# One load of the output weights in 30 KB rows instead of fifteen pieces in 2 KB rows, with O gathered through GpSimd

## The chip, the cores, the metric

One core of one Trainium2 chip. The metric is the device time of one execution in microseconds (us). Most executions of a kernel agree within 0.3%. The "span" is the stretch that the profile covers; it is 1 to 2 us shorter than the time.

## The reference

Decode attention with a cache, then a gated feed-forward layer, two batch rows, bfloat16:

```python
# B=2, Sq=1, D=512, H=32 heads, Sk=8192 cached keys, Dh=128, F=1376
q = layernorm(x) @ wq                       # wq 512 x 4096
p = softmax(q @ k_cache^T * Dh**-0.5)       # k_cache, v_cache: 2 x 32 x 8192 x 128, 134 MB each
h = x + (p @ v_cache) @ wo                  # wo 4096 x 512, 4.2 MB
n = layernorm(h)
out = h + (relu(n @ W_gate) * (n @ W_up)) @ W_down
```

Nearly all bytes are the two caches. wo is 1.5% of the 281 MB, and it is wo that the change is about.

## The kernel before

Work goes in 32 "pairs" p (two heads of one batch row: one K tile and one V tile of 4 MB each, four slots in SBUF). Two pairs make a round g. For each pair, VectorE computes 96 of the 128 columns of scores (a product of K with the query, then halving additions); TensorE computes the other 32 by transposing K and multiplying with the query. ScalarE takes exponentials, TensorE multiplies with V. After each round, O of two heads is normalized and multiplied with 256 rows of wo. SyncE issues all loads, in one queue, as slots come free. The loads of a round, and the GpSimd copy that lets TensorE begin on a K tile:

```python
def load_wo(dst, g, sem):                   # 256 KB: 128 partitions, 2 KB each
    nc.sync.dma_start(dst[:], A_wo[2*g*Dh:2*(g+1)*Dh].rearrange("(p r) n -> p (r n)", r=2)).then_inc(sem, 16)
...
for p in range(NP):
    ...
    if p < P0:                              # P0 = the last pair but one
        nc.gpsimd.wait_ge(slot_sem[s], 16 * (g + 1))                  # K has landed
    nc.gpsimd.tensor_copy(out=q2c[p % 2][:], in_=q2[:, p]).then_inc(g2p, 1)   # TensorE waits for g2p
    ...
    dve.wait((slot_sem[s], 16 * (g + 1)), t_q_b)
    t_dm[p] = dve.run(nc.vector.tensor_tensor(out=prod[:, 0:jd, :], in0=k_t[:, 0:jd, :], in1=qv, op=ALU.mult))
    ...                                     # 4 halving additions between prod and tb, 1 reduction
    if p + 2 < NP:
        sp.wait(t_dm[p], tokp("pt", p, NG - 1))     # product and transposes of K(p) done
        load(s, A_k_cache, p + 2)
    if p % 2 == 1 and 1 <= g < NI:
        sp.wait(tok("om", g))
        load_wo(wo_cur, g, sem_wo)
    if p < NP - 4:
        sp.wait(tokp("pv", p))
        load((2 * p + 1) % 4, A_v_cache, p + 2)
```

After the last V come the loads of W_up, W_gate and W_down, and the kernel ends with a serial stretch: collect O, project with the last 256 rows of wo, layernorm, up, gate, down, output.

The softmax here doesn't subtract the row's maximum and nothing guards it: scores larger than these inputs give would overflow.

## Time and profile before

| what | value | where it is read |
|---|---|---|
| time | 662.9 us (662.8 to 663.1) | runs |
| span | 661.1 us | profile |
| busy: DMA queue / DVE / PE | 99.3% / 70% / 51% | page, parts 3 and 1 |
| DMA rate | 425 GB/s mean, about 430 in the middle | page, part 2 |
| granted TensorE clock | mostly 0.5 or 0.6 of full speed after the first 83 us | page, part 2 |

The page of the kernel before: busy time of the engines, the DMA rows of the 40 slices (tenths of busy time; GB/s), the hardware queue, and the two lines of the chain that ended last.

```profile
PE 338.1 (51%) x3685; PEld 219.1 (33%) x3685; DVE 465.6 (70%) x274; ACT 198.3 (30%) x416; POOL 194.1 (29%) x48
...
DMA  9999999999999999999999999999999999999996
GB/s 381 429 426 439 421 438 429 434 424 430 438 430 428 428 430 440 427 431 428 428 438 430 428 430 430 437 427 428 429 434 432 432 424 432 436 419 442 430 419 276
...
q1 hardware_dynamic: 12664, 281.06, 99.3%
...
DMA 71%; DVE 23%; PE 2%; POOL 2%; ACT 1%; issue 0%; SPq 0%; DVEq 0%; POOLq 0%
DMA slot<-in_A_k_cache_dram 64%; DVE prod L474 14%; DVE tb L482 6%; DMA slot<-in_B_W_gate_dram 4%; DVE prod L482 3%; POOL q2c L463 2%; DMA slot<-in_A_wq_dram 2%; PE T L325 1%; PE W L229 1%; ACT q_b L276 0%; PE O L271 0%; ACT kT L499 0%; PE 
```

The queue is full from the first slice to the last but one. The last line lists whose work the chain is made of: besides the K tiles, the load of W_gate has 4% of it, so the end of the program hangs on that load. What shortens the span must therefore shorten the queue's work, or the stretch after the queue has run empty.

The timeline of the kernel before (start, duration, engine, line, operation, out<-in; in brackets how long the engine had been idle and what ended that): three products of K tiles, and two query copies.

```profile
221.96 6.56 DVE L474 TENSOR_TENSOR prod<-slot,q_b 128x12288 bf16<-128x12288 bf16 x1 [5.78 <-DMA slot<-in_A_k_cache_dram]
222.06 6.51 POOL L463 COPY q2c<-q 128x8 bf16<-128x8 bf16 x1 [13.59 <-DMA slot<-in_A_k_cache_dram]
...
241.40 6.56 DVE L474 TENSOR_TENSOR prod<-slot,q_b 128x12288 bf16<-128x12288 bf16 x1 [2.54 <-DMA slot<-in_A_k_cache_dram]
...
261.50 6.56 DVE L474 TENSOR_TENSOR prod<-slot,q_b 128x12288 bf16<-128x12288 bf16 x1 [5.78 <-DMA slot<-in_A_k_cache_dram]
```
```profile
24.10 0.19 POOL L463 COPY q2c<-q 128x8 bf16<-128x8 bf16 x1 [19.24 <-DMA slot<-in_A_k_cache_dram]
```

A product starts when its K tile lands. From 221.96 to 241.40 the queue moved V and K, 8.39 MB in 19.44 us: 431 GB/s. From 241.40 to 261.50 it moved V, K and one piece of wo, and took 20.10 us. The piece cost 0.66 us. The second fence shows a query copy with VectorE at rest, 0.19 us. Beside the product it takes 6.51 us and ends when the product ends.

The end of the kernel before: the load of W_gate (KB, and us from issue to landing), then from its timeline the last matmuls that can run without W_gate, the gate matmuls, and the last operation of VectorE.

```profile
slot<-in_B_W_gate_dram SPq DMA_DIRECT2D x1, 1376.0 KB, 29.1
...
654.15 0.41 PE L595 MATMUL T<-ident,hb 128*2 128x32 bf16 x16
...
654.71 1.71 PE L584 MATMUL O<-d_b,slot 128*128 128x2 bf16 x44
...
658.36 0.35 DVE L643 SCALAR_TENSOR_TENSOR o_r<-O,r,h_r 128x128 bf16<-128x128 f32 x1 [1.37 <-PE O L636]
```

W_gate lands at 654.66 (issued at 625.56, and 29.1 us to landing). TensorE had finished everything else at 654.56. So the serial work of the end is hidden behind the queue, but by only 0.1 us in this profile.

### The profile page before, as it was taken

The numbers are of one execution on the slowest core, as the hardware profiler recorded it, in microseconds if no ns is written. First come the engines' busy times: TensorE is split into PE (matmuls) and PEld (weight loads), VectorE is DVE, ScalarE is ACT, GpSimd is POOL, SyncE is SP. The second block draws the span as 40 slices with busy tenths as digits, with TensorE's granted clock in tenths as the row PEclk, the third lists the DMA queues.
The fourth block names the chain that finished last, engine by engine and source line by source line (L and its number), as shares of the span: only waits on it lengthen the run. The fifth ranks groups of instructions, "written<-read, shape, count | busy, mean of one in ns | idle before, by whom it ended". The sixth has DMA issues, their size and how long they took to land.

```text
span 661.1 us, 8515 instructions
## 1 busy us (share of the span) xinstructions
PE 338.1 (51%) x3685; PEld 219.1 (33%) x3685; DVE 465.6 (70%) x274; ACT 198.3 (30%) x416; POOL 194.1 (29%) x48
## 2 busy tenths in 40 slices
PE   2635554446545445644536545445653536544767
PEld 2413432324333233432314333223432314333444
DVE  1766787767688676787767688676788767688681
ACT  0603332223332123332223332123332213332360
POOL 2021333332233331233332133332233332134000
PEclk9999966656555566555655555566555665556556
DMA  9999999999999999999999999999999999999996
GB/s 381 429 426 439 421 438 429 434 424 430 438 430 428 428 430 440 427 431 428 428 438 430 428 430 430 437 427 428 429 434 432 432 424 432 436 419 442 430 419 276
DMA packets 12689, 281.22 MB, mean 425 GB/s; under 512 B 1442, under 2 KB 1540, under 8 KB 3972
## 3 DMA queue, kind: packets, MB, share of 16 engines
q1 hardware_dynamic: 12664, 281.06, 99.3%
q8 instruction: 6, 0.10, 0.1%
q14 instruction: 7, 0.06, 0.0%
q10 hardware_dynamic: 12, 0.00, 0.0%
HBM read 281.05 MB, written 0.00 MB: 425 GB/s over the span
## 4 chain that ended last, share of the span: by engine, by line
DMA 71%; DVE 23%; PE 2%; POOL 2%; ACT 1%; issue 0%; SPq 0%; DVEq 0%; POOLq 0%
DMA slot<-in_A_k_cache_dram 64%; DVE prod L474 14%; DVE tb L482 6%; DMA slot<-in_B_W_gate_dram 4%; DVE prod L482 3%; POOL q2c L463 2%; DMA slot<-in_A_wq_dram 2%; PE T L325 1%; PE W L229 1%; ACT q_b L276 0%; PE O L271 0%; ACT kT L499 0%; PE O L584 0%; PE O L636 0%; PE S L313 0%
## 5 line engine op out<-in xcount | busy, mean ns | idle before, releaser
L463 POOL COPY q2c<-q 128x8 bf16<-128x8 bf16 x32 | 190.4, 5949 | 415.5 <-DMA slot<-in_A_k_cache_dram 384.2
L474 DVE TENSOR_TENSOR prod<-slot,q_b 128x12288 bf16<-128x12288 bf16 (+1 forms) x32 | 207.7, 6491 | 128.9 <-DMA slot<-in_A_k_cache_dram 127.3
L325 PE MATMUL T<-ident_f,slot 128*128 128x128 f32 x528 | 136.5, 426 | 219.8 <-POOL q2c L463 217.8
L499 ACT ACTIVATE kT<-T 128x1024 bf16<-128x1024 bf16 x132 | 131.4, 1022 | 388.9 <-PE T L325 385.0
L325 PEld LDWEIGHTS T<-ident_f,slot 128*128 128x128 f32 x528 | 98.3, 219 | 233.6 <-POOL q2c L463 231.4
L482 DVE TENSOR_TENSOR tb<-prod 128x6144 bf16<-128x6144 bf16 (+1 forms) x64 | 136.8, 2137 | 2.2
L343 PE MATMUL O<-slot,e 128*32 128x512 bf16 x1024 | 115.5, 615 | 18.7 <-ACT e L429 18.7
L482 DVE TENSOR_TENSOR prod<-tb 128x3072 bf16<-128x3072 bf16 (+1 forms) x64 | 73.4, 1148 | 2.2
L313 PE MATMUL S<-q2c,kT 128*128 128x4 bf16 x1056 | 50.3, 170 | 37.7 <-ACT kT L499 37.7
L313 PEld LDWEIGHTS S<-q2c,kT 128*128 128x128 bf16 x1056 | 44.0, 108 | 67.8 <-ACT kT L499 65.8
L343 PEld LDWEIGHTS O<-slot,e 128*32 128x32 bf16 x1024 | 32.4, 132 | 76.6 <-issue 53.8
L355 PE MATMUL Ob<-sel,os_sb 128*64 128x2 f32 x544 | 31.1, 245 | 26.2 <-ACT os_sb L507 25.5
L355 PEld LDWEIGHTS Ob<-sel,os_sb 128*64 128x64 f32 x544 | 29.7, 217 | 28.1 <-ACT os_sb L507 26.9
L487 DVE TENSOR_REDUCE scores<-prod 128x96 f32<-128x768 bf16 (+1 forms) x32 | 30.2, 945 | 1.1
L429 ACT ACTIVATE e<-scores 64x96 bf16<-64x96 f32 (+1 forms) x64 | 19.6, 307 | 22.8 <-DVE scores L487 22.1
L438 DVE TENSOR_REDUCE zr<-Ob 128x2 f32<-128x4 f32 x15 | 2.4, 162 | 28.1 <-PE Ob L355 28.1
L429 ACT ACTIVATE e<-S 64x32 bf16<-64x32 f32 (+1 forms) x64 | 13.0, 204 | 14.8 <-PE S L313 14.5
L429 ACT ACTIVATION_READ_ACCUMULATOR e<-S 64x1 f32 x64 | 12.9, 201 | 0.7
L429 ACT ACTIVATION_READ_ACCUMULATOR e<-scores 64x1 f32 x64 | 11.8, 184 | 0.0
L507 ACT ACTIVATE os_sb<-O 128x512 f32<-128x512 f32 x16 | 9.6, 597 | 0.4
L276 ACT ACTIVATE q_b<-O 128x512 bf16<-128x512 f32 x8 | 4.3, 595 | 16.9 <-PE O L271 16.9
L234 DVE CAST qT<-W 128x64 bf16<-128x64 f32 x1 | 0.2, 224 | 11.2 <-PE W L229 11.2
(74 smaller groups left out, 72.0 us busy)
## 6 DMA issues: line engine op xcount, KB each, us to landing
slot<-in_A_k_cache_dram SPq DMA_DIRECT2D x32, 4096.0 KB, 28.1
slot<-in_A_v_cache_dram SPq DMA_DIRECT2D x31, 4096.0 KB, 31.3
slot<-in_A_wq_dram SPq DMA_DIRECT2D x1, 4096.0 KB, 12.3
slot<-in_A_v_cache_dram SPq DMA_DIRECT2D x2, 2048.0 KB, 29.6
wo_cur<-in_A_wo_dram SPq DMA_DIRECT2D x15, 256.0 KB, 27.0
slot<-in_B_W_up_dram SPq DMA_DIRECT2D x1, 1376.0 KB, 26.2
slot<-in_B_W_gate_dram SPq DMA_DIRECT2D x1, 1376.0 KB, 29.1
slot<-in_B_W_down_dram SPq DMA_DIRECT2D x2, 512.0 KB, 30.3
```

The costliest lines, as they stand in the source:

```text
L229: i = nc.tensor.matmul(Wp[:, h * B:(h + 1) * B], lhsT=wq[:, c, h * Dh:(h + 1) * Dh], rhs=lT[:, c * B:(c + 1) * B], start=(c == 0), stop=(c ...
L313: i = nc.tensor.matmul(Sp[p % 2][:, 2 * jj:2 * jj + 4], lhsT=kv_[:, k, r, :], rhs=q2c[p % 2][:, r, :], start=(r == 0), stop=(r == 1))
L325: i = nc.tensor.transpose(Tp[g % 2][:, k * 128:(k + 1) * 128], k_t[:, j:j + 2, :].rearrange("p j d -> p (j d)").bitcast(F32), ident_f[:])
L343: i = nc.tensor.matmul(Op[0][c:c + 32, :], lhsT=e_t[q][:, j // VJ, :], rhs=v_t[:, j:j + VJ, :].rearrange("p j d -> p (j d)"), start=(q == ...
L355: i = nc.tensor.matmul(Ob[64 * a_:64 * a_ + 64, B * r:B * r + B], lhsT=os_sb[:].rearrange("p (j d r) -> p j r d", j=VJ, r=2)[:, jj, r, :], ...
L429: i = nc.scalar.activation(out=e_t[q][h, j0 // VJ:j1 // VJ, 8 * q:8 * q + 8].rearrange("p g (j a) -> p g j a", a=2)[:, :, :, a], in_=src(h ...
L463: nc.gpsimd.tensor_copy(out=q2c[p % 2][:], in_=q2[:, p]).then_inc(g2p, 1)
L474: t_dm[p] = dve.run(nc.vector.tensor_tensor(out=prod[:, 0:jd, :], in0=k_t[:, 0:jd, :], in1=qv, op=ALU.mult))
L482: dve.run(nc.vector.tensor_tensor(out=o, in0=cur[:, :, 0:half], in1=cur[:, :, half:w], op=ALU.add))
L487: t_s[p] = dve.run(nc.vector.tensor_reduce(out=sc[:, 0:jd], in_=cur, axis=AX.X, op=ALU.add))
L499: to_pe(nc.scalar.activation(out=kT[gg % 2][:], in_=Tp[gg % 2][:].bitcast(BF16), func=ACT.Copy))
L507: to_pe(nc.scalar.activation(out=os_sb[:], in_=Op[0][:], func=ACT.Copy))
```

## The change

The intent: fifteen pieces of wo in 2 KB rows become one load near the start, 128 rows of 30 KB. Row p of that load holds rows 30p to 30p+29 of wo, so O has to be brought into the same order. GpSimd "spreads" O of each round into a masked tile, TensorE gathers it in PSUM over all rounds with a selector, and 30 matmuls of 512 columns do the whole projection near the end. Also: queries are copied a pair ahead, the halving additions work in place, O comes out of 4 matmuls instead of 16, and the program no longer stands in a block of its own. The core of the diff, cut:

```diff
-                    if p % 2 == 1 and 1 <= g < NI:
-                        sp.wait(tok("om", g))
-                        load_wo(wo_cur, g, sem_wo)
+                nc.sync.dma_start(                                # once, after the second V
+                    X[:], A_wo[0:128 * DR].rearrange("(p r) n -> p (r n)", r=DR)).then_inc(sem_wo, 16)
@@ GpSimd, per round
+                def o_spread(g):
+                    pool.wait(t_oc[g], tok("og", g))
+                    if g >= 1:
+                        ...
+                        pool.run(nc.gpsimd.memset(O_l[:, :, :, p0:min(p1 + NM, 128)], 0.0))
+                        pool.last()
+                    for a in range(2):
+                        p0, off = first(2 * g + a)
+                        n = min(NM, 128 - p0)
+                        nc.gpsimd.tensor_copy(out=rsel[:, a, :], in_=rows[:, DR - off:2 * DR - off])
+                        i = nc.gpsimd.tensor_tensor(out=O_l[:, a, :, p0:p0 + n], in0=O_cur..., in1=mask..., op=ALU.mult)
+                    i.then_inc(l2p, 1)
@@ the order on TensorE at the end
-                k_part(tail, P0, 0, ((slot_sem[0], 256), (g2p, 1)))
-                collect(tail, 6)
-                k_part(tail, P1, 7, ((slot_sem[2], 256), (g2p, 2)))
-                o_proj(tail, wo_cur)
+                collect(tail, 1)
+                k_part(tail, P0, 1, ((slot_sem[0], 256), (g2p, 1)))
+                o_gather(tail)                                    # waits for the last spread
+                for r in range(DR):                               # 30 matmuls of 512 columns
+                    i = nc.tensor.matmul(Op[1][32 * (r % 4):32 * (r % 4) + B, :],
+                        lhsT=O_all[:, r, :], rhs=X[:, r * D:(r + 1) * D], start=(r < 4), stop=(r >= DR - 4))
+                k_part(tail, P1, 8, ((slot_sem[2], 256), (g2p, 2)))
+                for c in range(DC):                               # into the sum for h
+                    nc.tensor.matmul(Wp[:, c * B:(c + 1) * B], lhsT=os_sb..., rhs=sel2[:], ...)
                 pv(tail, P0, ...)
@@ VectorE, at the last pair but one
+                    if p == P0:
+                        o_norm(g - 1, t_ob_loop)
                     dve.wait((slot_sem[s], 16 * (g + 1)), t_q_b)
@@ the program
-        with nc.Block() as block:
-            @block.sync
-            def _(eng):
+        if True:
+            def program():
```

## The prediction

> **What bounds it now.** The profile's slices show the DMA engines at 90% or more in every slice but the last; the hardware queue carries 99.3% of them, 425 GB/s over the span, and the chain of waits is 71% DMA. DVE is 70% busy, PE 51%. In the timeline, K tiles land 19.44 us apart where only V and K were queued between (8.39 MB: 431 GB/s, 9.72 us per tile), and 20.10 us apart where one 256 KB piece of wo was queued as well. So a piece costs 0.66 us of queue time, against 0.61 us at the tiles' rate.
>
> **Removed.** 15 wo loads of 2 KB rows: 15 x 0.66 = 9.9 us of queue. The skill ("Perfetto Trace Analysis", DMA Optimizations) warns of transfers under 2 KB; here 2 KB rows cost only 8% more.
> **Added to the queue.** One load of 3.93 MB in 30 KB rows: 9.1 us at 431 GB/s (estimate). The three small loads of the last W_down rows merely move to the front. Net for DMA: -0.8 us; without its own block the program may start about 0.2 us sooner. In the loop, queries copied ahead let PE start at K's landing rather than after the 6.5 us copy on GpSimd, but no load is waiting for that (issue to landing is 28 us): no gain. GpSimd's spread there falls into the 3 to 5 us in which DVE is idle.
>
> **The tail decides.** Before, it is nearly balanced: V's last half lands by 647.8, PV, projection and up-projection end at 654.6, W_gate lands at 654.7. The change puts new serial work after the last K but one: normalize, GpSimd spread (memset, copy, multiply, copy, multiply), gather matmuls, evacuation, 30 matmuls of 512 columns, and PE runs them in order before the last pair's 8 transposed groups. I expect normalize to end about 0.8 us after that K lands, as the product on DVE starts. The skill ("SBUF — State Buffer", Who interferes with whom) says a DVE instruction with two SBUF inputs excludes a GpSimd instruction reading SBUF; the trace agrees: the query copy takes 0.19 us free and 6.51 us beside the product. With one GpSimd read let in per DVE instruction (6.56, 3.36, 1.76, 0.96 us), the spread ends at about 630. Gather and evacuation 0.7 us; 30 matmuls 3.3 us (32 PV matmuls take 3.6). The last pair's groups, whose evacuation began at 632.6, begin at about 635; PV of the last pair ends near 652.2 rather than 649.1. The new 4-matmul collection gives back about 0.7 us. W_gate's matmuls then start about 2 us late, after its data. Estimate: span +1.8 us, less 0.2 at the start. If GpSimd gets in sooner, the tail stays hidden and the kernel gains 0.8 to 1 us.
>
> **Predicted:** 663.6 us, 661.2 to 666.6; faster by over 2%: 0.01; within 2%: 0.97; slower: 0.02.
>
> **Signs.** DMA packets fall by about 1,900 at equal bytes; K tiles all land 19.4 to 19.5 us apart; the query copies no longer take 6.5 us or lead PE's transposes; DMA busy unchanged. In the timeline of the last 45 us: the last spread's GpSimd operations end with DVE's instructions, the gather waits for them until about 630, and the gate matmuls start with no DMA wait before them. If instead the chain still ends DMA W_gate, gate, down, output, the tail was hidden and the time is about 661.8.
>
> **What would make it wrong.** The tail term: the spread free of the lock (faster), or each of its operations waiting for two DVE instructions (2 us slower); PE's granted clock in the tail (0.5 to 0.72 before) changing the 30 matmuls. In-place halving on DVE slower than into a second buffer: 5 us of slack per pair hides it in the loop. The 30 KB rows not at full rate.

## The result

663.38 us (662.6 to 663.84, 4 runs) against 663.01 us (662.82 to 663.17, 4 runs): ratio 1.0004, 95% interval 0.9987 to 1.0022. No measurable difference, and inside the predicted range.

The two nearly equal times hide several changes of about a microsecond each, as the profile after shows. From its page, in the order of the lines shown of before, and then three groups of instructions (busy us, mean ns of one, idle before and what ended it):

```profile
PE 333.3 (50%) x3220; PEld 203.4 (31%) x3220; DVE 465.0 (70%) x277; ACT 198.6 (30%) x418; POOL 34.0 (5%) x126
...
GB/s 381 430 415 428 444 421 432 436 422 442 426 432 438 425 432 432 428 440 426 432 434 424 440 427 430 438 428 434 432 427 434 430 432 432 430 437 430 426 424 257
...
q1 hardware_dynamic: 10760, 281.06, 99.1%
...
DMA 76%; DVE 16%; PE 4%; POOL 2%; ACT 1%; issue 0%; SPq 0%; DVEq 0%
DMA slot<-in_A_k_cache_dram 76%; DVE prod L516 15%; POOL rsel L490 1%; PE O L367 1%; DVE prod L522 1%; ACT kT L547 1%; PE O L421 1%; PE T L349 0%; PE Ob L377 0%; PE W L428 0%; PE S L659 0%; PE O L659 0%; PE S L337 0%; PE O L711 0%; DVE scor
...
L499 POOL COPY q2c<-q 128x8 bf16<-128x8 bf16 x32 | 9.1, 284 | 235.1 <-DMA slot<-in_A_v_cache_dram 221.2
L485 POOL MEMSET O_l<- 128x40 bf16 (+1 forms) x14 | 1.9, 136 | 325.9 <-DVE O_cur L470 325.9
L490 POOL COPY rsel<-rows 128x30 bf16<-128x30 bf16 x30 | 15.6, 520 | 34.4 <-DVE O_cur L470 33.5
```

W_gate has gone from the chain: its DMA share is all K tiles, and after the last of these it runs over GpSimd (rsel L490) and TensorE, whose share rose from 2 to 4%. GpSimd's busy time fell from 194 to 34 us, because a query copy now takes 0.28 us in the mean. DMA moved the same bytes in 10,787 packets instead of 12,689. Two of the last three lines belong to the spread: the memset, which only writes, has a mean of 0.14 us, and the copy, which reads, of 0.52 us. That mean hides two kinds: in the loop a copy takes 0.21 us, and only the last two of the thirty, shown below, take 6.46 and 3.33 us.

Three products in the middle of the changed kernel:

```profile
267.70 6.56 DVE L516 TENSOR_TENSOR prod<-slot,q_b 128x12288 bf16<-128x12288 bf16 x1 [5.10 <-DMA slot<-in_A_k_cache_dram]
...
287.15 6.56 DVE L516 TENSOR_TENSOR prod<-slot,q_b 128x12288 bf16<-128x12288 bf16 x1 [4.65 <-DMA slot<-in_A_k_cache_dram]
...
306.57 6.56 DVE L516 TENSOR_TENSOR prod<-slot,q_b 128x12288 bf16<-128x12288 bf16 x1 [5.11 <-DMA slot<-in_A_k_cache_dram]
```

K tiles land 19.45 and 19.42 us apart: the pieces are gone from the queue. From the third K tile to the thirtieth (73.35 to 598.46 us) the mean distance is 19.45 us, before it was 19.73 (64.68 to 597.37).

The end of the changed kernel, the load of W_gate and then lines of its timeline:

```profile
slot<-in_B_W_gate_dram SPq DMA_DIRECT2D x1, 1376.0 KB, 27.9
...
618.57 0.16 DVE L470 TENSOR_TENSOR O_cur<-Ob,zi 128x4 bf16<-128x4 f32 x1
...
618.79 0.15 POOL L485 MEMSET O_l<- 128x44 bf16 x1 [10.30 <-DVE O_cur L470]
618.84 6.56 DVE L516 TENSOR_TENSOR prod<-slot,q_b 128x12288 bf16<-128x12288 bf16 x1
619.01 6.46 POOL L490 COPY rsel<-rows 128x30 bf16<-128x30 bf16 x1
...
625.42 0.21 POOL L491 TENSOR_TENSOR O_l<-O_cur,mask 128x12 bf16<-128x12 bf16 x1
...
625.43 6.83 DVE L522 TENSOR_TENSOR prod<-prod 128x6144 bf16<-128x6144 bf16 x4
625.57 3.33 POOL L490 COPY rsel<-rows 128x30 bf16<-128x30 bf16 x1
...
628.86 0.21 POOL L491 TENSOR_TENSOR O_l<-O_cur,mask 128x10 bf16<-128x10 bf16 x1
...
629.12 0.29 PE L390 MATMUL O<-rsel,O_l 128*128 128x30 bf16 x4 [6.16 <-POOL O_l L491]
...
629.75 3.58 PE L421 MATMUL O<-X,O_all 128*2 128x512 bf16 x30 [0.33 <-ACT O_all L575]
...
642.48 2.01 PE L428 MATMUL W<-sel,os_sb 128*128 128x2 f32 x8
...
648.23 1.90 PE L367 MATMUL O<-slot,e 128*16 128x512 bf16 x32
...
655.39 1.72 PE L659 MATMUL O<-d_b,slot 128*128 128x2 bf16 x44
```

VectorE finishes the normalized O at 618.73 and starts the product at 618.84. GpSimd's memset, begun 0.05 us before the product, runs into it without delay to either. Its copy, which reads SBUF, starts at 619.01 and ends at 625.47, with the product. A multiply slips through. The second copy starts at 625.57 and ends at 628.90, which is the length of the first halving addition. The last multiply ends at 629.07, and only then can TensorE gather: 10.3 us after normalize, where a spread in the loop took 0.9. The 30 matmuls, the last pair's transposes, PV and the rest follow one after the other. W_gate was issued at 625.80 and landed 27.9 us later, at 653.7, so 1.0 us sooner than before. Its matmuls start at 655.39, and the line shows no wait for a transfer: they are 1.7 us late.

### The profile page after: what moved, and what is told of

Read it like the earlier page. It is cut to its first block, busy times and chain, and to the rows that moved or that the text cites. A ratio compares the mean times of both kernels' runs of the same rounds, so it can differ in the third digit from the quotient of the medians.

```text
span 661.4 us, 7674 instructions
## 1 busy us (share of the span) xinstructions
PE 333.3 (50%) x3220; PEld 203.4 (31%) x3220; DVE 465.0 (70%) x277; ACT 198.6 (30%) x418; POOL 34.0 (5%) x126
## 2 busy tenths in 40 slices
DMA packets 10787, 281.23 MB, mean 425 GB/s; under 512 B 1202, under 2 KB 1556, under 8 KB 1940
## 4 chain that ended last, share of the span: by engine, by line
DMA 76%; DVE 16%; PE 4%; POOL 2%; ACT 1%; issue 0%; SPq 0%; DVEq 0%
DMA slot<-in_A_k_cache_dram 76%; DVE prod L516 15%; POOL rsel L490 1%; PE O L367 1%; DVE prod L522 1%; ACT kT L547 1%; PE O L421 1%; PE T L349 0%; PE Ob L377 0%; PE W L428 0%; PE S L659 0%; PE O L659 0%; PE S L337 0%; PE O L711 0%; DVE scores L527 0%
## 5 line engine op out<-in xcount | busy, mean ns | idle before, releaser
L522 DVE TENSOR_TENSOR prod<-prod 128x6144 bf16<-128x6144 bf16 (+4 forms) x128 | 210.3, 1643 | 4.4
L367 PE MATMUL O<-slot,e 128*16 128x512 bf16 x1024 | 118.5, 616 | 185.3 <-ACT e L454 129.7
L349 PE MATMUL T<-ident_f,slot 128*128 128x128 f32 x528 | 121.8, 390 | 51.6 <-POOLq L534 51.6
L349 PEld LDWEIGHTS T<-ident_f,slot 128*128 128x128 f32 x528 | 87.9, 200 | 66.8 <-issue 66.7
L367 PEld LDWEIGHTS O<-slot,e 128*16 128x16 bf16 x1024 | 25.9, 112 | 251.8 <-ACT e L454 157.6
L377 PE MATMUL Ob<-sel,os_sb 128*128 128x4 f32 x136 | 30.2, 345 | 24.9 <-ACT os_sb L562 24.2
L377 PEld LDWEIGHTS Ob<-sel,os_sb 128*128 128x128 f32 x136 | 28.7, 312 | 26.8 <-ACT os_sb L562 25.6
L499 POOL COPY q2c<-q 128x8 bf16<-128x8 bf16 x32 | 9.1, 284 | 235.1 <-DMA slot<-in_A_v_cache_dram 221.2
L490 POOL COPY rsel<-rows 128x30 bf16<-128x30 bf16 x30 | 15.6, 520 | 34.4 <-DVE O_cur L470 33.5
L383 PEld LDWEIGHTS Ob<-zs,ones_f 128*128 128x128 f32 x30 | 7.0, 292 | 12.8 <-issue 12.8
## 6 DMA issues: line engine op xcount, KB each, us to landing
slot<-in_B_W_gate_dram SPq DMA_DIRECT2D x1, 1376.0 KB, 27.9
```

Of the source, the lines that this page charges most:

```text
L349: i = nc.tensor.transpose(Tp[g % 2][:, k * 128:(k + 1) * 128], k_t[:, j:j + 2, :].rearrange("p j d -> p (j d)").bitcast(F32), ident_f[:])
L367: i = nc.tensor.matmul(Op[0][c:c + 16, :], lhsT=e_t[q][:, j // VJ, :], rhs=v_t[:, j:j + VJ, :].rearrange("p j d -> p (j d)"), start=(q == ...
L377: i = nc.tensor.matmul(Ob[:, 0:4], lhsT=os_sb[:, jj * Dh:(jj + 1) * Dh], rhs=sel[:, 4 * jj:4 * jj + 4], start=(jj == 0), stop=(jj == VJ - 1))
L490: nc.gpsimd.tensor_copy(out=rsel[:, a, :], in_=rows[:, DR - off:2 * DR - off])
L522: dve.run(nc.vector.tensor_tensor(out=prod[:, 0:jd, 0:half], in0=prod[:, 0:jd, 0:half], in1=prod[:, 0:jd, half:w], op=ALU.add))
```

## The experiments

Seven kernels, all correct. The kernel before had medians of 662.93 and 662.91 us beside them.

### 1. The changed kernel again

No edit; it gives the spread of its times and a second profile on the chip of experiments 2 to 4.

> The changed kernel again, unedited, for its spread and another profile. Theory A (the end of the span is now set by serial work on TensorE, started late by the GpSimd spread, which waits for VectorE's product): 663.0 to 664 us, spread over runs of about 1 us, because the granted clock in the last 45 us now matters; whatever the profile's clock, the gate matmuls start 1 us or more after W_gate landed. Theory B (the end is still set by the transfers, and the row change simply gave nothing): 663 us with a spread of 0.3 us, like the kernel before.

Measured: 663.0 us (662.67 to 663.47), ratio 1.0000 [0.9987, 1.0014]. In this profile W_gate landed at 653.66 (issued 626.46, 27.2 us) and its matmuls started at 655.78: 2.1 us late. That is theory A's sign. The spread of the times, which was to tell the theories apart as well, does not: 0.8 us here, and one run of the kernel before in the same rounds was 663.91.

### 2. VectorE's product waits for the spread

```diff
                     if p == P0:
                         o_norm(g - 1, t_ob_loop)
+                        nc.vector.wait_ge(l2p, 1)
```

> VectorE's product with the last K but one waits until the last spread is done, so GpSimd never meets its lock; all TensorE work stays. Theory A: the spread ends about 1.2 us after normalize (it took 0.9 us in the loop) instead of 10.4 us, the product is 1 us later, the 30 matmuls run before the last K lands, the gate matmuls wait for W_gate again, and the time is 661.8 to 662.3 us, ratio to before 0.998 to 0.999. Theory B: no change, 663.4 us. Theory C (the added TensorE work itself, 30 matmuls and the 2 us of the small W matmuls, is what makes the tail late, lock or not): at most 1 us of gain, gate matmuls still late.

Measured: 661.85 us (660.9 to 662.11), ratio 0.9978 [0.9965, 0.9992]. The timeline of the spread and of what came to hold the end instead:

```profile
619.82 0.21 POOL L490 COPY rsel<-rows 128x30 bf16<-128x30 bf16 x1
...
619.98 0.21 POOL L491 TENSOR_TENSOR O_l<-O_cur,mask 128x12 bf16<-128x12 bf16 x1
620.12 0.21 POOL L490 COPY rsel<-rows 128x30 bf16<-128x30 bf16 x1
620.29 0.21 POOL L491 TENSOR_TENSOR O_l<-O_cur,mask 128x10 bf16<-128x10 bf16 x1
...
620.53 6.56 DVE L517 TENSOR_TENSOR prod<-slot,q_b 128x12288 bf16<-128x12288 bf16 x1 [0.99 <-POOL O_l L491]
```
```profile
645.65 0.59 PE L383 MATMUL S<-zs,ones_f 128*128 128x8 f32 x2 [2.04 <-ACT e L454]
```

The same four reading operations that took 10 us now take 0.7. All TensorE work was left in, and the kernel gained 1.1 us over experiment 1 (means 661.75 and 663.09: 1.3; the ranges do not overlap), so theory B falls. Theory C is not yet out: it allowed a gain of up to 1 us with the gate matmuls still late. Experiment 3 decides about it. One part of theory A's expectation missed: the gate matmuls still started at 654.89, with W_gate there at 653.8. The product was 1 us later, and so were the scores that VectorE makes for the last pair. TensorE waited 2.0 us for their exponentials (L383) before it could go on. The wait had moved from GpSimd to VectorE.

### 3. The selector copies go first

The two copies of a spread build the selector and do not read O, so they need not wait for it.

```diff
-                    pool.wait(t_oc[g], tok("og", g))
+                    pool.wait(tok("og", g))
                     if g >= 1:
                         ...                                       # memset
+                    for a in range(2):
+                        off = first(2 * g + a)[1]
+                        nc.gpsimd.tensor_copy(out=rsel[:, a, :], in_=rows[:, DR - off:2 * DR - off])
+                    pool.last()
+                    pool.wait(t_oc[g])
                     for a in range(2):
                         p0, off = first(2 * g + a)
-                        nc.gpsimd.tensor_copy(...)
                         i = nc.gpsimd.tensor_tensor(...)          # multiply
```

> The two selector copies of a spread move ahead of the wait for the normalized O (they do not read it), so only the two multiplies are left behind the lock. Theory A: the last multiply lands just after the product, about 6.8 us after normalize instead of 10.4, so 3.4 us sooner; the 30 matmuls end at about 630 instead of 633; of the 1.7 us by which the gate matmuls came late all or nearly all goes: 661.9 to 662.5 us. Theory B: 663.4 us.

Measured: 660.98 us (660.82 to 661.15), ratio 0.9969 [0.9955, 0.9982]. The spread in the timeline, and the gate matmuls:

```profile
608.31 1.93 POOL L488 COPY rsel<-rows 128x30 bf16<-128x30 bf16 x2
...
619.49 6.56 DVE L519 TENSOR_TENSOR prod<-slot,q_b 128x12288 bf16<-128x12288 bf16 x1
619.54 6.74 POOL L494 TENSOR_TENSOR O_l<-O_cur,mask 128x12 bf16<-128x12 bf16 x2 [9.31 <-DVE O_cur L470]
...
626.34 0.29 PE L390 MATMUL O<-rsel,O_l 128*128 128x30 bf16 x4 [1.52 <-POOL O_l L494]
```
```profile
652.92 0.41 PE L673 MATMUL T<-ident,hb 128*2 128x32 bf16 x16
...
653.61 1.71 PE L662 MATMUL O<-d_b,slot 128*128 128x2 bf16 x44 [0.28 <-DMA slot<-in_B_W_gate_dram]
```

The copies are done at 610, long before O. Both multiplies, merged into one line here, start with the product and end at 626.28, 0.2 us after it. The gather is 3.4 us nearer to normalize than in experiment 1, as expected. The gate matmuls wait for the transfer again, with TensorE done 0.3 us before. The kernel is back at the queue's limit, and it beats both kernels. All TensorE work is still in, so theory C falls as well: the added work makes the end late only together with the wait. The time is also 0.9 us below the lower end of my expectation. Counted from the kernel before, W_gate's earlier start of 1.1 us alone gives 661.8; experiment 5 shows where the rest comes from.

### 4. The 30 matmuls twice

```diff
-                for r in range(DR):
+                for r in list(range(DR)) + list(range(DR)):
                     i = nc.tensor.matmul(Op[1][32 * (r % 4):...], ..., start=(r < 4), stop=(r >= DR - 4))
```

> The 30 wo matmuls run twice (the second pass starts its groups anew, so the result stays right). Theory A: the tail has no slack left, so the time rises by the whole 3.3 to 3.6 us, to about 666.8 us. Theory B: there is slack, and the time stays within 1 us of 663.4.

Measured: 665.38 us (664.88 to 667.09), ratio 1.0040 [1.0025, 1.0055], so 2.4 us over experiment 1 by the medians. TensorE's lines (PEld is its weight load):

```profile
630.44 5.75 PE L421 MATMUL O<-X,O_all 128*2 128x512 bf16 x60 [0.33 <-ACT O_all L575]
...
634.66 1.02 PEld L421 LDWEIGHTS O<-X,O_all 128*2 128x2 bf16 x16 [0.29 <-issue]
...
658.29 1.71 PE L659 MATMUL O<-d_b,slot 128*128 128x2 bf16 x44
```

Sixty matmuls took 5.75 us where thirty took 3.58, so the doubling added 2.17 us, and the gate matmuls moved by 2.5 (655.78 to 658.29). All of what was added came out at the end: no slack. The expectation of 3.3 to 3.6 us missed the granted clock. The first 44 weight loads come mostly in fours, 0.43 us apart (0.11 us each), until 634.66; then, after 4.2 us of steady work, the last 16 take 1.02 us (0.06 us each). This agrees with the Trainium skill ("TensorE: Matmul & The Clock Gate", Part 1), which puts the transition at about 4 us into sustained matmul activity.

### 5. The kernel before without its block

```diff
-        with nc.Block() as block:
-            @block.sync
-            def _(eng):
+        if True:
+            def program():
                 ...
+            program()
```

> The kernel before, with only its block taken away. The profiled spans of before leave 1.8 us to the measured time, those of the changed kernel 1.2 us. If the block is the cause, this kernel's span stays at 661.1 us or falls by up to 0.4, the remainder falls to 1.2 to 1.3, and the time is 662.2 to 662.5 us (ratio 0.999). If the rest of the change is the cause: 662.9 us.

Measured: 662.27 us (661.86 to 662.38), ratio 0.9988 [0.9974, 1.0001]. Over five runs the time exceeds the span by 1.26 to 1.38 us; in the nine runs of the kernel before beside it, by 1.79 to 1.91. The spans are 660.6 to 661.1. So about 0.5 us of the 0.6 us lies outside the span. The profiles show a second piece inside it: from the start of VectorE's last operation to the end of the span there are 2.74 us in the kernel before and 2.39 us here (2.37 in the changed kernel, 2.35 in experiment 3), so 0.35 us. The runs' spans show less of it (medians 660.9 against 661.1). The interval of the ratio just touches 1, so the total is not quite settled by it alone; the step in the remainder, which no run of either kernel crosses, is clear.

### 6. The kernel before with the query copied ahead

```diff
-                    if p < P0:
-                        nc.gpsimd.wait_ge(slot_sem[s], 16 * (g + 1))
-                    nc.gpsimd.tensor_copy(out=q2c[p % 2][:], in_=q2[:, p]).then_inc(g2p, 1)
+                    pool.run(nc.gpsimd.tensor_copy(out=q2c[p % 2][:], in_=q2[:, p]))
+                    if p < P0:
+                        nc.gpsimd.wait_ge(slot_sem[s], 16 * (g + 1))
+                    pool.last()
+                    nc.gpsimd.sem_inc(g2p, 1)
```

> The kernel before, with only the copy of the queries moved ahead of the wait for the K tile (the go-ahead to TensorE stays behind that wait). My theory: TensorE starts its transposes at the landing of K instead of 6.6 us later, GpSimd's 6.5 us copies become 0.2 us, and the time stays within 0.5 us of 662.9, for no transfer was waiting. Rival (the late TensorE start held up the slots and so the transfers): at least 1 us faster.

Measured: 663.1 us (662.99 to 663.14), ratio 1.0000 [0.9986, 1.0013]. The timeline of one pair:

```profile
261.22 1.97 PE L325 MATMUL T<-ident_f,slot 128*128 128x128 f32 x8 [1.97 <-POOLq L465]
...
271.32 1.60 POOL L461 COPY q2c<-q 128x8 bf16<-128x8 bf16 x1 [18.49 <-PE Ob L355]
```

The product of that pair starts at 261.13, the transposes now at 261.22; in the kernel before they came 6.66 us after the product (221.96 to 228.62). TensorE starts 6.6 us sooner in almost every pair and the time does not move. The copies did not all become 0.2 us, as I had expected: they now run beside the additions, with a median of 0.64 us and up to 1.60.

### 7. The one load, in 2 KB rows

```diff
-                nc.sync.dma_start(X[:], A_wo[0:128 * DR].rearrange("(p r) n -> p (r n)", r=DR)).then_inc(sem_wo, 16)
+                for k in range(DR // 2):
+                    nc.sync.dma_start(X[:, 2 * k * D:(2 * k + 2) * D],
+                        A_wo[0:128 * DR].rearrange("(p r) n -> p (r n)", r=DR)[:, 2 * k * D:(2 * k + 2) * D]).then_inc(sem_wo, 16)
...
-                nc.tensor.wait_ge(sem_wo, 16)
+                nc.tensor.wait_ge(sem_wo, 16 * (DR // 2))
```

> The changed kernel with its one wo load cut into 15 loads of 2 KB rows at the same place in the queue: same bytes, only the rows differ. Row-size theory (2 KB rows cost 0.05 us per 256 KB, so 8%): the third K tile, queued behind them, starts its product at 74.0 to 74.2 us instead of 73.3, and every later tile is later by the same; the time rises by up to 0.8 us, to 663.4 to 664.2. If rows of 2 KB cost nothing, 73.3 us and no change; if they are what costs the pieces most of their time in the queue, over 75 us.

Measured: 664.13 us (662.95 to 664.56), ratio 1.0011 [0.9996, 1.0027]. The third product in the timelines of this kernel and of the changed kernel:

```profile
74.32 6.56 DVE L518 TENSOR_TENSOR prod<-slot,q_b 128x12288 bf16<-128x12288 bf16 x1 [15.28 <-DMA slot<-in_A_k_cache_dram]
```
```profile
73.35 6.56 DVE L516 TENSOR_TENSOR prod<-slot,q_b 128x12288 bf16<-128x12288 bf16 x1 [14.22 <-DMA slot<-in_A_k_cache_dram]
```

The tile is 0.97 us later (1.03 against experiment 1's profile), and stays so: 599.40 against 598.46 for the thirtieth. The same 3.93 MB thus cost about 1 us more in 2 KB rows, 0.065 us per piece, where I had estimated 0.05.

The edit changes two things, the rows and the number of loads, and SyncE needed 38.2 us to issue the fifteen, so that the next K tile was issued at 55.51 us instead of 32.30. The trace speaks for the rows: from 44.8 to 73.35 us the queue stayed full (DMA share 1.02, in the changed kernel 1.00), and in the traces' records of single packets a 2 KB packet of these loads takes 88 ns (85 in the kernel before), while the changed kernel's 30 KB packet takes 1142 ns, 76 ns for each 2 KB. No run cuts the load without shortening its rows.

## Why the prediction was right

The time, 663.38 us, was 0.2 us from the 663.6 predicted (663.0 in experiment 1), and the mechanism was the predicted one. That the number is so near is partly luck. The recorded sum does not say what its +1.8 us is counted from: on the 662.9 us of before it gives 664.5, and only on the hidden tail's 661.8 us does it give 663.6. And its own steps made the tail later than "about 2 us": PV was to end at 652.2, and the 5.4 us from there to TensorE's readiness for the gate matmuls, as before, less 0.7 lead to 656.9, 3 us after a W_gate landing at 653.9. Measured were 655.4 and 655.8. Point by point:

- **The queue gains 0.8 us: right.** W_gate landed 1.0 us sooner (653.7 against 654.66). Experiment 7, with 2 KB rows again, has W_gate at 654.73 (issued 627.53, 27.2 us), so the gain goes with the rows.
- **The earlier start of TensorE is worth nothing: right.** Experiment 6 isolates it.
- **The tail is what decides, through GpSimd's wait for VectorE: right.** The gate matmuls came 1.7 and 2.1 us after their data in two profiles; I had said about 2. Experiment 4 shows that nothing from the 30 matmuls on has slack. Experiment 3, which only moves two copies, removes the whole lateness, and experiment 2 confirms the cause from the other side.
- **The spread ends at about 630: nearly right (629.07), by errors that partly cancel.** I let in one GpSimd read per VectorE instruction, so four waits. A copy and a multiply passed together at each boundary, so it waited for only two instructions. On the other side, I had taken all of the queue's gain as made by the last K tiles. Two of the fifteen pieces were in the queue behind the thirtieth K tile, so that tile landed 1.1 us later than before, not sooner. In experiment 1 normalize was later still (619.40 instead of 618.73), because the collection before it took 1.87 us instead of 1.06.
- **The collection gives back 0.7 us: wrong.** Collecting at the end took 1.05 us after and 1.13 us before: the loads are fewer but wider (8 of 128 columns instead of 32 of 64). I also left out the matmuls that add the projection to h, 2.0 us (L428). Against this stood TensorE's clock: the view by stretches has it at 0.87 of full speed from 637 to 647 us, before at 0.50 in the same stretch, and PV of the last pair ended at 650.13, not 652.2.
- **The start gains 0.2 us without the block: wrong in place and size.** The first load was issued at 0.81 us, before at 0.74. The gain is about 0.5 us outside the span and up to 0.35 us at its end (experiment 5). That is why the time rose by only 0.4 us while the spans rose from 661.1 to between 661.4 and 662.6, and why the hidden-tail version runs at 661.0 and not at the 661.8 that I named.

So the change was worth about 1.0 us in the queue and 0.6 to 0.9 us through the block, and one wait in the last 45 us took about 2.0 us of it back (663.0 us in experiment 1, 660.98 in experiment 3). Without that wait the kernel takes 660.98 us, 0.3% less than before. What share of the lateness in each run belongs to the clock and not to the wait stays open: the profiles have different clocks in the tail, and I had no way to fix it.

## What to carry to other kernels

Where a queue is full from end to end, work moved off it pays only as long as the serial end stays hidden; here 0.1 to 0.3 us of slack was all there was, so an added wait of 6 us in front of TensorE was worth asking about before anything else. Let GpSimd do whatever does not depend on the newest data before it waits for it: here the reads that it started beside a long VectorE instruction with two SBUF inputs ended only with that instruction (6.46 us instead of 0.21). And when a small change gives nothing, undo its parts one at a time: gains and losses of a microsecond may sit side by side.

## What the Trainium skill lacked or had wrong

- "SBUF — State Buffer", Who interferes with whom: it says that a VectorE instruction with two SBUF inputs contends with a GpSimd instruction that reads SBUF, not with one that only writes it; its section "Summary: rules for kernel authors" adds that the second to issue is blocked until the first has finished. The runs agree: the copy took 6.46 us beside the product, and the memset 0.15 us, though it had begun 0.05 us before the product. The page does not say how many queued GpSimd instructions pass when the lock comes free. Here a second one went through right behind the first, and the four additions of VectorE took 6.83 us instead of 6.74.
- "Perfetto Trace Analysis", DMA Optimizations: it calls the per-transfer overhead of small DMAs significant and advises steps such as 2 KB to 4 KB or 8 KB, without a size for the cost; "DMA: Bandwidth & Descriptors" has no measured cost of 2 KB rows on this chip either. Here 2 KB rows cost about 1 us more for 3.93 MB, which takes 9.1 us at the tiles' 431 GB/s (an estimate): about 11%.
- No page that I read has it: a program in a block of its own had 1.8 us of time outside the profiled span, without it 1.3.
- "TensorE: Matmul & The Clock Gate", Part 1: agreed with the runs (4.2 us of steady work before the faster pace).
